# Token records with the head innermost, 576 bytes stored and gathered instead of 784

## The chip, the core and the metric

One core of a Trainium2 chip runs the whole program. The metric is the device time of one execution in microseconds: 197.95 us is the median of three runs of the kernel before (197.73 to 199.84). TensorE (PE) multiplies matrices and transposes, VectorE (DVE) and ScalarE (ACT) work on elements, GpSimd (POOL) issues indirect transfers here, and SyncE (SP) issues plain ones. DMA queues move data between the memory of the chip (DRAM) and the core's own memory (SBUF); TensorE writes its results to PSUM, 128 partitions of eight banks.

## The reference

A linear attention over random sketches is followed by a mixture of experts with one expert per token. There are 4 batches of 1088 tokens, 4 heads of 32 numbers, 64 sketch features, so 4352 tokens of 128 numbers; 8 experts of hidden width 1024. All is float32.

```
def phi(x):                                   # 8 x 8 = 64 features per head
    a = einsum('rd,bhsd->bhsr', S1, x); b = einsum('rd,bhsd->bhsr', S2, x)
    return outer(a, b)
q_p, k_p = phi(q), phi(k)
kv = einsum('bhsf,bhsd->bhfd', k_p, v); z = sum(k_p, axis=2)
attn = einsum('bhsf,bhfd->bhsd', q_p, kv) / (einsum('bhsf,bhf->bhs', q_p, z) + 1e-06)
x = attn as [4352, 128]
logits = x @ w_gate; e = argmax(logits); gate = softmax(logits)[e]
eom = sigmoid(x @ w_output_gate)
out = gate * eom[e] * (relu(x @ w1[e]) @ w2[e])
```

## The kernel before, in words

Tokens go in 34 chunks of 128, in nine groups (eight of four chunks, the last of two), and the groups in three routes of 12, 12 and 10 chunks. For each group TensorE makes the sketches, VectorE the products, and TensorE either adds the keys' part up per batch (`sums`) or turns the queries' part (`turned`) and multiplies it with the batch's sums (`attend`). Next to the 32 sums of a head stand the denominator and 16 gate logits, so that a head has VG = 49 numbers and a token W = 4 x 49 = 196. ScalarE copies these from PSUM into `xall` (`below`: one copy per pair of heads at L595, the denominator with its epsilon at L596). VectorE then takes the reciprocal of the denominators in place (L608), scales the logits (L610) and adds the four heads up (L612, L613): `shared`. When a route is whole, VectorE chooses experts and slots (`choose_first`, `choose_second`, `slot`), ScalarE makes the exponentials, VectorE the weight of the token (`weigh`), and `label` (L739) writes that weight into the record over its first logit, at column VZ = 33. `store` (L743) sends the route's records, all 196 columns of each token, to a DRAM table `xt` of 784 bytes per token.

The expert part works in tiles of 128 rows of one expert. GpSimd gathers a tile's records from `xt` by a list of row numbers into a buffer of `xin` (`fetch`, L858); a gather needs the stores of the routes that it may read and the list (`index_fixed`, which ends at L717). VectorE multiplies the sums by the reciprocal (`divide`, L868, into `xdiv`), TensorE turns the tile (`turn`, L872), VectorE copies it (`turn_copy`), TensorE multiplies up (`up`, L885), ScalarE or VectorE takes the positive part (`relu`), TensorE multiplies down (`down`, L899), ScalarE scales by the record's weight (`scale`, L902), and GpSimd scatters the rows to the output (`give`, L998). Sixteen tiles are done alone, after the first and second route. Then three tiles per expert are done as one group of up to 384 columns (`group_divide` L929 and L931, `group_up` L951, `group_down` L968 and so on), and a few last tiles follow, as many as there are rows left over, with weights fetched into buffers that are free by then.

The order of all this is written out by hand: the list `ORDER` names every step, and each engine runs its own steps in that order, each waiting by semaphores for what it needs. Names that matter below: `Rg` is `below` of group g (ScalarE), `Xg` is `shared`, `CAi`, `CBi`, `WEi`, `LAi`, `STi` lead from a route's logits to its store, `IXm` ends a list of rows, `Ft` is a gather, `XDt` a division, `TNt` a turn, `UPt` a multiplication up. Around the first route ScalarE has `R1`, `R2` one behind the other, and VectorE has `X1 X2 CA0 Mq.5 CB0 Mk.5 Pk.5 Mq.6 WE0 LA0` (the `M` and `P` steps belong to later groups' sketches). TensorE has `TN0`, the first turn, right behind the sums of group 5. PSUM buffers go round: two pairs of banks (`ps_w`) serve sketches, turned queries, the sums for `below`, and the multiplications up, so `UP2` takes the buffer that `R8` gives back.

Of the kernel before, what the change touches and what calls it, by code (L numbers as in the profile page):

```python
# [12 lines left out]
F32 = mybir.dt.float32  # L13
# [4 lines left out]
ACTF = mybir.ActivationFunctionType  # L18
# [6 lines left out]
TS = 128  # L25
# [33 lines left out]
JOINED = ()  # L59
# [28 lines left out]
def kernel(  # L88
# [27 lines left out]
    W = H * VG  # L116
    JT = (N + (len(MARKS) + 1) * TS) // TS
# [8 lines left out]

    xt = dram.tile([N, W], F32, tag="xt", name="xt")

# [173 lines left out]
    xins = const("xin", [TS, NX + 3, W])  # L302
# [72 lines left out]
    for t in xin:  # L375
        blank(t, 2, W // 2)
# [7 lines left out]
    lgs = Ring("lg", 1, [128, 16 * max([1] + [len(x) for x in JOINED]), 2 * E])  # L384
# [199 lines left out]
    def sums_of(g):  # L584
        cs = groups[g]
        return xall[:, cs[0]:cs[-1] + 1].rearrange("p c (k x) -> p (c k) x", x=VG)
# [4 lines left out]
    def below(g):  # L591
        n = 2 * len(groups[g])
        out = sums_of(g).rearrange("p (k h) x -> p h k x", h=2)
        for b in range(2):
            nc.scalar.copy(out[:, b], now["nd", g][:, b, :n])  # L595
        nc.scalar.activation(out[:, :, :, D], now["nd", g][:, :, :n, D], ACTF.Identity, bias=eps)  # L596
        ps_w.back(("nd", g))

    def shared(g):
        i = route_of[g]  # L600
        cs = range(groups[joined(g)[0]][0], groups[g][-1] + 1)
        n = len(cs)
        at = cs[0] - routes[i][0]
        if at == 0:
            now["x", i], now["L", i] = xall[:, routes[i][0]:routes[i][-1] + 1], Ls()
        raw = xall[:, cs[0]:cs[-1] + 1].rearrange("p c (k x) -> p (c k) x", x=VG)
        rc = raw[:, :, D]
        nc.vector.reciprocal(rc, rc)  # L608
        lg = lgs()[:, :4 * n]
        nc.vector.tensor_mul(lg, raw[:, :, VZ:], rc.unsqueeze(2).to_broadcast((128, 4 * n, 2 * E)))  # L610
        pairs = lg.rearrange("p (c a k) e -> p c a k e", a=2, k=2)
        nc.vector.tensor_add(pairs[:, :, 0], pairs[:, :, 0], pairs[:, :, 1])  # L612
        nc.vector.tensor_add(now["L", i][:, at:at + n], pairs[:, :, 0, 0], pairs[:, :, 0, 1])  # L613
# [123 lines left out]
    def label(i):  # L737
        n, x = len(routes[i]), now["x", i]
        nc.vector.tensor_mul(x[:, :n, VZ], now["co", i][:, :n], now["ey", i][:, :n, E + 1])  # L739

    def store(i):
        a, n = routes[i][0], len(routes[i])
        nc.sync.dma_start(xt[a * 128:(a + n) * 128].rearrange("(c p) w -> p c w", p=128), now["x", i])  # L743
# [122 lines left out]
    def divide(t):  # L866
        x = xin[room(t)].rearrange("p (k x) -> p k x", x=VG)
        nc.vector.tensor_mul(xdiv[t % 2].rearrange("p (k d) -> p k d", d=D), x[:, :, :D], x[:, :, D].unsqueeze(2).to_broadcast((TS, H, D)))  # L868
# [32 lines left out]
    def scale(t):  # L901
        nc.scalar.activation(at_ys(t), now["y", t], ACTF.Copy, scale=xin[room(t)][:, VZ:VZ + 1])  # L902
        ps_y.back(t)
# [22 lines left out]
    def group_divide(e):  # L926
        x = xins[:, room(first_of(e)):room(first_of(e)) + TG]
        heads = x.rearrange("p t (k x) -> p t k x", x=VG)
        nc.vector.tensor_mul(wide_div.rearrange("p (t k d) -> p t k d", t=TG, d=D), heads[:, :, :, :D],  # L929
                             heads[:, :, :, D].unsqueeze(3).to_broadcast((TS, TG, H, D)))  # L930
        nc.vector.tensor_copy(scales[e % 3], x[:, :, VZ])  # L931
# [235 lines left out]
    def scale_last(t):  # L1167
        nc.vector.tensor_scalar_mul(at_ys(t), now["y", t], xin[room(t)][:, VZ:VZ + 1])
        ps_y.back(t)
# [95 lines left out]
```

## Time and profile before

| | |
|---|---|
| runs | 197.95 us median (197.73 to 199.84) |
| profiled execution | 200.12 us, of which the span of the trace is 198.4 |
| mean granted TensorE clock | 0.983 |
| busy: PE, PEld | 187.1, 169.6 us (94%, 85%) |
| busy: DVE, ACT, POOL | 110.1, 72.8, 89.4 us (56%, 37%, 45%) |
| DMA | 31.11 MB, mean 157 GB/s |
| indirect queue (gathers and scatters) | 5.65 MB, 9.8% of 16 engines |
| SP's queue (q1, with the stores) | 16.44 MB, 24.1% |

PE is the time of matrix instructions, PEld that of loading their stationary operand. Times in the trace count from the start of the span. A group of instructions is named by its line, its engine and the tiles that it writes and reads. The chain of waits is followed back from the last instruction of the run, at each step to what released it; where an engine was simply busy, the step is the instruction before it on the same engine.

### The profile page before, as it was taken

What the parts mean: (1) busy time and instruction counts of PE and PEld (TensorE: products, weight loads), DVE (VectorE), ACT (ScalarE), POOL (GpSimd) and SP (SyncE); (2) the same over time, 40 slices, a digit from 0 to 9 for tenths busy, and PEclk for the clock granted to TensorE, in tenths of its full rate; (3) what the DMA queues carried; (4) which work ended last, traced back from release to release, by engine and by line L of the source; (5) the groups of instructions that cost most, each with busy time, mean ns of one, the idle gap of its engine ahead of it and who ended that gap; (6) DMA issues with size and microseconds to landing.
All of it is one profiled execution on the core that took longest, in us unless ns stands there. A gap on an engine that the chain in (4) does not pass through costs nothing.

```text
span 198.4 us, 5595 instructions
## 1 busy us (share of the span) xinstructions
PE 187.1 (94%) x2207; PEld 169.6 (85%) x2207; DVE 110.1 (56%) x299; ACT 72.8 (37%) x173; POOL 89.4 (45%) x117
## 2 busy tenths in 40 slices
PE   7999999795899999999999999999999999999980
PEld 6999998695899999999999996777988876788980
DVE  5579889984856848548453842342642806155230
ACT  7526685635257634333022304031242121223300
POOL 1830000007806105776057877758677375145071
PEclk9999999999799999999999999999999999999996
DMA  5969875354588699556999422122111110001010
GB/s 153 335 190 326 282 241 167 99 151 149 143 304 324 188 342 274 188 180 159 405 423 420 160 59 63 49 57 72 41 45 47 24 44 13 18 17 43 14 33 28
DMA packets 14878, 31.11 MB, mean 157 GB/s; under 512 B 2553, under 2 KB 7815, under 8 KB 14064
## 3 DMA queue, kind: packets, MB, share of 16 engines
q1 hardware_dynamic: 9328, 16.44, 24.1%
q10 hardware_dynamic: 2320, 8.39, 13.1%
q0 software_dynamic: 3184, 5.65, 9.8%
q8 instruction: 31, 0.51, 1.1%
q14 instruction: 15, 0.12, 0.2%
HBM read 25.53 MB, written 5.90 MB: 158 GB/s over the span
## 4 chain that ended last, share of the span: by engine, by line
DMA 44%; PE 40%; issue 7%; POOL 4%; DVE 2%; ACT 1%; POOLq 1%; DVEq 0%
DMA xin<-xt,putf 18%; DMA out_dram<-ys,putf 14%; PE w L885 11%; DMA xin<-xt,putfar 8%; PE t L431 6%; PE y L899 6%; PE acc L899 4%; DMA xt<-xall 4%; PE w L556 4%; PE w L579 3%; PE acc L497 3%; POOL xin L858 3%; PE w L417 2%; POOL out_dram L998 1%; PE t L872 1%
## 5 line engine op out<-in xcount | busy, mean ns | idle before, releaser
L858 POOL DMA_INDIRECT xin<-xt,putf x36 | 39.2, 1089 | 52.3 <-ACT ab L452 33.5
L998 POOL DMA_INDIRECT out_dram<-ys,putf x36 | 36.6, 1017 | 42.7 <-ACT ys L902 12.2
L885 PE MATMUL w<-xsT,wt 128*128 128x128 f32 x256 | 32.4, 284 | 0.0
L951 PE MATMUL w<-vt,wt 128*128 128x256 f32 (+5 forms) x128 | 32.3, 396 | 0.0
L885 PEld LDWEIGHTS w<-xsT,wt 128*128 128x128 f32 x256 | 31.2, 201 | 0.0
L951 PEld LDWEIGHTS w<-vt,wt 128*128 128x128 f32 x128 | 22.7, 190 | 6.0 <-DVE kT L957 0.4
L957 DVE TENSOR_SCALAR kT<-w 128x768 f32<-128x768 f32 x8 | 7.7, 958 | 32.9 <-PE w L951 32.9
L890 ACT ACTIVATE hT<-w 128x1024 f32<-128x1024 f32 x13 | 13.3, 1022 | 20.9 <-PE w L885 20.9
L899 PE MATMUL y<-wt,hT 128*128 128x128 f32 x144 | 17.7, 276 | 0.0
L899 PEld LDWEIGHTS y<-wt,hT 128*128 128x128 f32 x144 | 16.8, 192 | 0.1
L968 PE MATMUL acc<-kT,wt 128*128 128x256 f32 (+5 forms) x64 | 16.2, 396 | 0.1
L968 PE MATMUL acc<-qT,wt 128*128 128x256 f32 (+5 forms) x64 | 16.0, 392 | 0.0
L972 ACT COPY kT<-acc 128x384 f32<-128x384 f32 x8 | 3.8, 478 | 31.0 <-PE acc L968 31.0
L968 PEld LDWEIGHTS acc<-kT,wt 128*128 128x128 f32 x64 | 11.6, 190 | 3.6 <-issue 0.7
L968 PEld LDWEIGHTS acc<-qT,wt 128*128 128x128 f32 x64 | 11.8, 190 | 2.9
L899 PE MATMUL acc<-wt,hT 128*128 128x128 f32 x112 | 13.7, 275 | 0.0
L899 PEld LDWEIGHTS acc<-wt,hT 128*128 128x128 f32 x112 | 13.1, 192 | 0.0
L959 ACT ACTIVATE qT<-w 128x768 f32<-128x768 f32 x8 | 6.5, 810 | 14.0 <-PE w L951 14.0
L878 DVE COPY xsT<-t 128x128 f32<-128x128 f32 x19 | 5.4, 286 | 10.8 <-PE t L872 10.8
L465 DVE TENSOR_TENSOR kp<-ab 128x1024 f32<-128x1024 f32 (+1 forms) x9 | 10.5, 1166 | 0.7 <-PE acc L497 0.3
L497 PE MATMUL acc<-vt,kp 128*64 128x33 f32 (+1 forms) x288 | 10.6, 224 | 0.0
L465 DVE TENSOR_TENSOR qp<-ab 128x1024 f32<-128x1024 f32 (+1 forms) x9 | 10.4, 1161 | 0.2
(182 smaller groups left out, 292.6 us busy)
## 6 DMA issues: line engine op xcount, KB each, us to landing
wt<-in_w_dram ACTq DMA_DIRECT2D x16, 512.0 KB, 5.6
xall<-in_w_dram SPq DMA_DIRECT2D x3, 1024.0 KB, 9.8
xt<-xall SPq DMA_DIRECT2D x2, 1176.0 KB, 9.7
vt<-in_v_dram SPq DMA_DIRECT2D x8, 260.0 KB, 4.5
kT<-in_k_dram SPq DMA_DIRECT2D x8, 256.0 KB, 4.3
qT<-in_q_dram SPq DMA_DIRECT2D x8, 256.0 KB, 4.4
qp<-in_w_dram SPq DMA_DIRECT2D x1, 1024.0 KB, 6.7
qpT<-in_w_dram SPq DMA_DIRECT2D x1, 1024.0 KB, 13.9
```

Source lines behind the costliest of these rows:

```text
L431: nc.tensor.matmul(ps[:, j].rearrange("p i x -> p (i x)"), src[:, j * 128:(j + 1) * 128], Sb.rearrange("p i h x -> p (i h x)"), start=True ...
L465: nc.vector.tensor_mul(res[:, :n], bview(av, [list(av.ap[1]), list(av.ap[2]), [0, r]]), bview(bv, [list(bv.ap[1]), [0, r], list(bv.ap[2])]))
L497: nc.tensor.matmul(now["acc", b][64 * h:64 * (h + 1), s], kp[p0:p0 + n, heads_at("k", g, j, s) + h].rearrange("s i j -> s (i j)"), now["v" ...
L556: nc.tensor.transpose(ps[:, :, x], block(x), ident)
L858: nc.gpsimd.indirect_dma_start(out=xin[room(t)], out_offset=None, in_=xt[:n, :], in_offset=bass.IndirectOffsetOnAxis(ap=index(t), axis=0), ...
L885: nc.tensor.matmul(ps[:, c], w[:, c], x[:, own(t)], start=True, stop=True)
L890: nc.scalar.activation(out, now["h", t], ACTF.Relu)
L899: nc.tensor.matmul(ps, h[:, c], w[:, c], start=(c == 0), stop=(c == FC - 1))
L951: nc.tensor.matmul(now["h", "g", e, s][:, c, :n], w[:, s * (FC // 4) + c], x[:, :n], start=True, stop=True)
L957: nc.vector.tensor_scalar_max(wide_h[s], src, 0.0)
L968: nc.tensor.matmul(ps[:, :n], w[:, c], wide_h[c // (FC // 4)][:, c % (FC // 4), :n], start=(c == 0), stop=(c == FC - 1))
L998: apart("out", nc.gpsimd.indirect_dma_start(out=out, out_offset=bass.IndirectOffsetOnAxis(ap=index(t), axis=0), in_=at_ys(t), in_offset=No ...
```

## The change

The record's 4 x 49 numbers are laid with the head innermost: column 4 x + k holds number x of head k. So the 128 sums come first, then the four denominators (RC, columns 128 to 131), then the 64 logits, and the weight of the token is written at column WZ = 132. A row of `xt` is cut at WR = 144 columns, 576 bytes, which holds the sums, the denominators and the weight, and eleven logits that nobody reads. `xall` keeps 196 columns per token, as the logits are needed there. The gather's buffers `xin` have 144 columns.

What follows from that: `below` writes each pair of heads to columns that lie four apart; the reciprocals of a chunk are four neighbours; `shared` multiplies blocks of 16 x 4 and adds over the innermost index; `divide` and `group_divide` read the sums of one head four columns apart; `store` takes 144 of the 196 columns. `turn`, `up` and everything behind them have the layout that they had. `ORDER` is not touched.

```diff
+    WR = 144
+    RC, WZ = slice(H * D, H * VZ), H * VZ
...
-    xt = dram.tile([N, W], F32, tag="xt", name="xt")
+    xt = dram.tile([N, WR], F32, tag="xt", name="xt")
...
-    xins = const("xin", [TS, NX + 3, W])
+    xins = const("xin", [TS, NX + 3, WR])
...
-        blank(t, 2, W // 2)
+        blank(t, 2, WR // 2)
...
 def sums_of(g):
-        return xall[:, cs[0]:cs[-1] + 1].rearrange("p c (k x) -> p (c k) x", x=VG)
+        return xall[:, cs[0]:cs[-1] + 1].rearrange("p c (x k) -> p c k x", k=H)
...
 def below(g):
-        out = sums_of(g).rearrange("p (k h) x -> p h k x", h=2)
+        out = sums_of(g).rearrange("p c (s h) x -> p h c s x", h=2)
+        src = now["nd", g][:, :, :n].rearrange("p h (c s) x -> p h c s x", s=2)
         for b in range(2):
-            nc.scalar.copy(out[:, b], now["nd", g][:, b, :n])
-        nc.scalar.activation(out[:, :, :, D], now["nd", g][:, :, :n, D], ACTF.Identity, bias=eps)
+            nc.scalar.copy(out[:, b], src[:, b])
+        nc.scalar.activation(out[:, :, :, :, D].rearrange("p h c s -> p c s h"), src[:, :, :, :, D].rearrange("p h c s -> p c s h"),
+                             ACTF.Identity, bias=eps)
...
 def shared(g):
-        raw = xall[:, cs[0]:cs[-1] + 1].rearrange("p c (k x) -> p (c k) x", x=VG)
+        raw = xall[:, cs[0]:cs[-1] + 1].rearrange("p c (x k) -> p c x k", k=H)
         rc = raw[:, :, D]
         nc.vector.reciprocal(rc, rc)
-        lg = lgs()[:, :4 * n]
-        nc.vector.tensor_mul(lg, raw[:, :, VZ:], rc.unsqueeze(2).to_broadcast((128, 4 * n, 2 * E)))
-        pairs = lg.rearrange("p (c a k) e -> p c a k e", a=2, k=2)
-        nc.vector.tensor_add(pairs[:, :, 0], pairs[:, :, 0], pairs[:, :, 1])
-        nc.vector.tensor_add(now["L", i][:, at:at + n], pairs[:, :, 0, 0], pairs[:, :, 0, 1])
+        lg = lgs()[:, :n]
+        nc.vector.tensor_mul(lg, raw[:, :, VZ:], rc.unsqueeze(2).to_broadcast((128, n, 2 * E, H)))
+        nc.vector.tensor_add(lg[:, :, :, :2], lg[:, :, :, :2], lg[:, :, :, 2:])
+        nc.vector.tensor_add(now["L", i][:, at:at + n], lg[:, :, :, 0], lg[:, :, :, 1])
...
 def label(i):
-        nc.vector.tensor_mul(x[:, :n, VZ], now["co", i][:, :n], now["ey", i][:, :n, E + 1])
+        nc.vector.tensor_mul(x[:, :n, WZ], now["co", i][:, :n], now["ey", i][:, :n, E + 1])
...
 def store(i):
-        nc.sync.dma_start(xt[a * 128:(a + n) * 128].rearrange("(c p) w -> p c w", p=128), now["x", i])
+        nc.sync.dma_start(xt[a * 128:(a + n) * 128].rearrange("(c p) w -> p c w", p=128), now["x", i][:, :, :WR])
...
 def divide(t):
-        x = xin[room(t)].rearrange("p (k x) -> p k x", x=VG)
-        nc.vector.tensor_mul(xdiv[t % 2].rearrange("p (k d) -> p k d", d=D), x[:, :, :D], x[:, :, D].unsqueeze(2).to_broadcast((TS, H, D)))
+        x = xin[room(t)]
+        nc.vector.tensor_mul(xdiv[t % 2].rearrange("p (k d) -> p k d", d=D), x[:, :H * D].rearrange("p (d k) -> p k d", k=H),
+                             x[:, RC].unsqueeze(2).to_broadcast((TS, H, D)))
...
 def group_divide(e):
-        heads = x.rearrange("p t (k x) -> p t k x", x=VG)
-        nc.vector.tensor_mul(wide_div.rearrange("p (t k d) -> p t k d", t=TG, d=D), heads[:, :, :, :D],
-                             heads[:, :, :, D].unsqueeze(3).to_broadcast((TS, TG, H, D)))
-        nc.vector.tensor_copy(scales[e % 3], x[:, :, VZ])
+        nc.vector.tensor_mul(wide_div.rearrange("p (t k d) -> p t k d", t=TG, d=D), x[:, :, :H * D].rearrange("p t (d k) -> p t k d", k=H),
+                             x[:, :, RC].unsqueeze(3).to_broadcast((TS, TG, H, D)))
+        nc.vector.tensor_copy(scales[e % 3], x[:, :, WZ])
```

The two scalings, `scale` and `scale_last`, take the weight from column WZ instead of VZ.

## Rows read from the trace of the kernel before

**Rows 1.** The page: busy tenths of TensorE in 40 slices.

```profile
PE   7999999795899999999999999999999999999980
```

**Rows 2.** The waits of PE: line, waited for: us in total, times, longest.

```profile
PE t L872 <- DVE xdiv L868: 2.8, 1, 2.8
```

**Rows 3.** The chain that ended last, at five places: start, us, what.

```profile
37.24 6.97 DMA xt<-xall
...
45.14 4.79 DMA xin<-xt,putf
...
50.30 0.33 PE t L872
...
51.85 5.17 PE w L885 x32
...
93.13 3.57 PE w L885 x32
```

**Rows 4.** The timeline, 27.8 to 43 us: start, us, engine, line, operation.

```profile
27.81 0.88 ACT L595 COPY xall<-w 128x392 f32<-128x392 f32 x2 [0.46 <-PE w L579]
...
28.89 0.87 ACT L595 COPY xall<-w 128x392 f32<-128x392 f32 x2
...
29.79 0.29 ACT L596 ACTIVATE xall<-w,eps 128x16 f32<-128x16 f32 x1
...
30.26 0.25 DVE L608 RECIPROCAL xall<-xall 128x16 f32<-128x16 f32 x1
...
34.63 1.23 DVE L465 TENSOR_TENSOR kp<-ab 128x1024 f32<-128x1024 f32 x1
...
36.22 0.27 DVE L732 TENSOR_REDUCE ss<-ey 128x12 f32<-128x108 f32 x1
...
42.73 0.17 DVE L717 SCALAR_TENSOR_TENSOR putf<-valf,nonef 128x8 int32<-128x8 f32 x1
```

**Rows 5.** Stretches: length, busy PE PEld DVE ACT POOL, granted clock, DMA share, GB/s.

```profile
38.40:39.60 1.20, 0.30 (x1) 0.11 (x1) 1.10 (x3) 1.13 (x7) 0.00 (x0) 1.00 0.98 319
...
30.00:40.00 10.00, 8.65 (x211) 7.93 (x211) 9.21 (x30) 6.19 (x20) 0.00 (x0) 1.00 0.43 133
...
100.00:105.00 5.00, 5.00 (x47) 5.00 (x46) 2.48 (x10) 0.98 (x3) 3.07 (x3) 1.00 1.01 419
...
51.80:52.00 0.20, 0.20 (x3) 0.20 (x2) 0.20 (x1) 0.20 (x1) 0.01 (x1) 0.50 0.00 0
```

**Rows 6.** Groups of instructions by line and form: count, busy us, mean ns.

```profile
L595 ACT COPY xall<-w 128x392 f32<-128x392 f32 x16 | 7.0, 493 | 4.7 <-PE w L579 4.7
...
L595 ACT COPY xall<-w 128x196 f32<-128x196 f32 x2 | 0.6, 328 | 1.2 <-PE w L579 1.2
...
L641 DVE TENSOR_TENSOR oh<-t,first 128x96 f32<-128x96 f32 x2 | 0.6, 317 | 0.0
...
L627 DVE TENSOR_TENSOR ex<-mx,L 128x96 f32<-128x96 f32 x2 | 0.5, 260 | 0.1
```

**Rows 7.** Instructions of single lines: ns shortest, median, longest, starts, forms.

```profile
L372 ACT COPY xin<-ys x12: 348/349/350, 3.8 to 6.6; 128x196 f32<-128x196 f32 x12
...
L636 ACT COPY oh<-bumped x2: 198/201/204, 59.3 to 74.9; 128x8 f32<-128x8 f32 x2
...
L596 ACT ACTIVATE xall<-w,eps x9: 273/289/291, 23.2 to 72.5; 128x16 f32<-128x16 f32 x8, 128x8 f32<-128x8 f32 x1
...
L715 DVE TENSOR_TENSOR valf<-rows_of x3: 173/174/200, 42.3 to 100.2; 128x8 f32<-128x8 f32 x2, 128x24 f32<-128x24 f32 x1
L715 DVE TENSOR_TENSOR valfar<-farboth x1: 192/192/192, 155.6 to 155.6; 128x32 f32<-128x32 f32 x1
...
L610 DVE TENSOR_TENSOR lg<-xall x9: 291/425/427, 23.8 to 75.8; 128x256 f32<-128x256 f32 x8, 128x128 f32<-128x128 f32 x1
```

**Rows 8.** The timeline at 63 us: a last copy and the weights after it.

```profile
63.34 0.27 ACT L596 ACTIVATE xall<-w,eps 128x8 f32<-128x8 f32 x1
...
63.66 1.86 PEld L885 LDWEIGHTS w<-xsT,wt 128*128 128x128 f32 x16
```

More of the change, by code (lines that the diff above doesn't have):

```diff
@@ L116 @@
     W = H * VG
+    WR = 144
+    RC, WZ = slice(H * D, H * VZ), H * VZ
+    assert WZ < WR <= W
     JT = (N + (len(MARKS) + 1) * TS) // TS
@@ L383 @@
     kvs = Ring("kv", 2, [128, 2, D])
-    lgs = Ring("lg", 1, [128, 16 * max([1] + [len(x) for x in JOINED]), 2 * E])
+    lgs = Ring("lg", 1, [128, 4 * max([1] + [len(x) for x in JOINED]), 2 * E, H])
     Ls = Ring("L", 2, [128, RG, 2 * E])
@@ L901, in scale @@
     def scale(t):
-        nc.scalar.activation(at_ys(t), now["y", t], ACTF.Copy, scale=xin[room(t)][:, VZ:VZ + 1])
+        nc.scalar.activation(at_ys(t), now["y", t], ACTF.Copy, scale=xin[room(t)][:, WZ:WZ + 1])
         ps_y.back(t)
@@ L1167, in scale_last @@
     def scale_last(t):
-        nc.vector.tensor_scalar_mul(at_ys(t), now["y", t], xin[room(t)][:, VZ:VZ + 1])
+        nc.vector.tensor_scalar_mul(at_ys(t), now["y", t], xin[room(t)][:, WZ:WZ + 1])
         ps_y.back(t)
```

## The prediction, made before the changed kernel was run

> **What bounds the kernel now.** I read the page first. TensorE's busy tenths stand at 9 in almost every slice; the one deep dip, a 5, is the slice from 44.6 to 49.6 us, with a 7 two slices before it [rows 1]. From 50 us on the tenths say that TensorE runs without a hole until the end, so work saved on another engine, a queue or a transfer after that point buys nothing unless TensorE waits for it. The waits of PE name the dip: 2.8 us, once, for the first division at L868 [rows 2]. The chain of waits says what was late: the first store of records is issued at 37.24 and lands 6.97 us later, the first gather is issued at 45.14 and takes 4.79 us, then come the division and, at 50.30, its transpose on TensorE [rows 3]. So a change to the records counts there, and there alone: where does the first transpose come, and does anything later make TensorE wait that did not wait before?
>
> The timeline shows what sets the issue of that store. It is not ScalarE's copies of group 3, which the chain names; that store holds groups 0 to 2. ScalarE copies group 1 from 27.81 and group 2 from 28.89, ending with L596 at 29.79 + 0.29 = 30.08; VectorE takes group 2 at 30.26 (L608), then goes on through the choice, a product (34.63) and the weights (36.22) to the label before the store [rows 4]. VectorE is busy 9.21 of these 10 us (the stretch 30 to 40) [rows 5], and its operations stand in one fixed order, so I count whatever delays L608 of group 2 as delaying the store by the same amount.
>
> **The change, part by part.**
>
> *The store, shorter.* Twelve chunks of 128 tokens are 1536 rows, 96 on each of 16 engines, 784 bytes before and 576 after. In the bulk of it the engines move 319 GB/s, all busy (share 0.98), where long weight rows move 419 [rows 5]. So one row takes 784 x 16 / 319 = 39.3 ns, of which 29.9 are bytes at the faster rate and 9.4 belong to the row. A row of 576 bytes then takes 22.0 + 9.4 = 31.4: 7.9 ns saved x 96 = 0.76 us; in proportion to bytes alone it is 1.0. I take 0.9. Ends: nothing, if the row is the price and not its bytes; and 0.265 x 6.97 = 1.8 if the whole time to landing shrinks, of which only 1.33 can be used, since the indices of the first gather are ready at 42.73 + 0.17 = 42.90 [rows 4] against the landing at 44.21.
>
> *The first gather, shorter.* 128 rows, 27 KB less, at 319 GB/s: 0.08, so -0.1 us; ends 0 and 0.3 (a share of the time in which it competes with a weight load). Gathers and stores after it are waited for by no TensorE instruction: nothing, covered by TensorE's own queue of work after 50 us [rows 1]; if that cover went, each would give another gain, not a loss.
>
> *ScalarE's copies out of the sums (L595).* The same 392 numbers per copy, but written 16 bytes apart, where before 49 lay side by side. No row shows a step of 16 bytes, so I bound it. ScalarE's ordinary price per number is (493 - 328) / 196 = 0.84 ns [rows 6]. Its writes in long steps: L636 writes 8 numbers 52 bytes apart in 201 ns, where the fixed part is 349 - 196 x 0.84 = 184, so 2.1 ns each; L596 goes from 273 to 289 ns for 8 more numbers in steps of 196 bytes, 2.0 each [rows 7]. That is 1.25 ns a number on top, from very small instructions. VectorE, per number: (425 - 291) / 128 = 1.05 ns [rows 7]; L715 over 24 numbers 20 bytes apart takes 200 ns, over 32 side by side 192 [rows 7], so 24 side by side would take 184, and the step costs 16 / 24 = 0.7 ns a number. L641, which writes 52 bytes apart, takes 317 where L627 takes 260, 0.6 a number over 96 [rows 6]. Ends: 0 and 1.25 (ScalarE's own rows); nothing below zero, since no number is left out. I take 0.7, because 20 bytes is the nearest step to 16. So a copy takes 0.27 us longer, a group's pair 0.55.
>
> [...] The rows at 20, 52 and 196 bytes agree that long steps cost; no row before the change shows 16.
>
> *What waits behind these copies.* Group 1's end moves by 0.55, group 2's by 1.10, to 31.18. VectorE's group 1 starts 0.55 later, so its group 2 could start at 30.81; ScalarE is later, at 31.18, which is +0.92. The last addition (L613) reads 64 numbers in steps of 16 bytes, +0.05. The store's issue: **+1.0** (ends 0 and, with 1.25 ns, copies of +0.49, group 2 done at 32.04, +1.8). TensorE waits somewhat too for the product at 34.63, later by the same 1.0; that moves its work toward the dip at 47.5, which has 2.8 us to give.
>
> *Divisions.* L868 reads its 128 numbers 16 bytes apart: +0.09 each. The first is on the path, and so is the second, whose transpose comes with no room; the other 17 and the eight wide ones (+0.27 each) run a tile ahead of TensorE, so nothing.
>
> *The last, short group.* At 63.34 + 0.27 = 63.61 ScalarE ends a short group, whose buffer TensorE fills from 63.66 [rows 8]: no more than 0.05 to spare. Two copies of 196 numbers, +0.14 each, make TensorE wait **+0.2** (at 1.25 ns, with the group behind it, up to 0.9).
>
> *Costed at nothing.* Blanking 144 columns instead of 196 (L372, ScalarE ahead of its first copies), the reciprocal and the product at L610 (runs of 64 and of 4 side by side), the label, the scales: same counts, off the path. No DMA is added or moved and no queue is reordered; SP and POOL issue what they did.
>
> Sum: +1.0 (issue) - 0.9 (store) - 0.1 (gather) + 0.1 + 0.1 (two divisions) + 0.2 (short group) = **+0.4 us**. It is made on the profiled execution, 200.12 us around a span of 198.4, so 200.5 there; that execution stands 2.2 above the median, 197.95, on which I put the same difference: **198.3 us**.
>
> **The rivals.**
>
> *The step is nearly free, a small gain.* The copies keep their 493 ns, so the issue stays at 37.24. For it: 16 bytes is shorter than any step in the rows. Against: 20 bytes costs 0.7. Then -0.9 - 0.1 = -1.0: 196.9.
>
> [...]
>
> *Slower: ScalarE becomes the bound ahead of the first store.* Its place is the copies of groups 1 and 2; its price 1.25 ns a number, +1.8 at the issue; and the store is bound by its rows, so it gives nothing back. With +0.2 for divisions and 0.5 for the short group: +2.5, 200.4. At that price it passes 1% when the store saves less than 0.5. For it: ScalarE's only rows with long steps, both at 2 ns. Against: they are instructions of 8 and 16 numbers, and 319 against 419 GB/s says that bytes weigh more than rows.
>
> *It does not do what it says*, the transfer being cut into the same packets by another rule: counted in the last case.
>
> **How the numbers follow.** Forecast 0.50, its own range 197.5 to 199.6 (price 0.4 to 1.25); small gain 0.17; clock holds 0.20; slower 0.13. Over or under 1%, 1.98 us, is about what a measurement tells from no change. So faster 0.20, same 0.67, slower 0.13. The range takes in the forecast, the small gain and the clock's case, and cuts off most of the slower case: 195.2 to 200.1.
>
> **What would show it.** L595 at about 760 ns (free: 493; dear: 980). The first store issued near 38.2 and landing in about 6.1 us. L868 near 370 ns. The PE wait for L868 near 2 us, and the clock after it at 0.50 or at 1.00. A TensorE wait of 0.2 before L885 at 63 us. I am wrong if L595 does not move, if the store's time does not, if the clock stays up, or if TensorE finds a new wait after 64 us.

## The result, and the profile after

The changed kernel takes 200.66 us (median of 19 runs, 198.43 to 204.0), the kernel before, measured beside it, 198.23 (19 runs, 196.62 to 200.01). The ratio is 1.011, with a 95% interval of 1.0077 to 1.0142: about 2.2 us lost. A ratio here compares only those executions of either kernel that lie within 1.5% of its fastest, so it isn't quite the ratio of the medians. The forecast was 198.3, and its range ended at 200.1.

The profile is of the slowest of these executions, 204.0 us around a span of 202.3. First its page, TensorE's busy tenths and its granted clock in 40 slices of 5.06 us each.

```profile
PE   7999997899999999999999999999999999999990
...
PEclk9999999955579999999999999999999999999998
```

The dip of [rows 1] is gone: there is no slice with a 5, but the ninth to twelfth slices hold a clock of 5 to 7, where TensorE is busy nine tenths of the time and more. Stretches of the same execution show where that begins (columns as in [rows 5]).

```profile
40.00:42.00 2.00, 1.36 (x39) 1.17 (x43) 1.90 (x5) 1.19 (x8) 0.00 (x0) 0.67 0.98 298
42.00:50.00 8.00, 8.00 (x138) 7.33 (x130) 4.69 (x11) 3.04 (x6) 2.80 (x2) 0.50 0.08 22
50.00:57.00 7.00, 7.00 (x134) 6.80 (x133) 3.45 (x12) 3.10 (x8) 5.24 (x5) 0.50 0.46 130
```

The clock is at 0.50 from about 41 to 57 us; before, it was at 1.00 over 40 to 50 us, until the wait was over, 0.91 over 50 to 52, and at 0.50 only behind it [rows 5]. So this execution is late early: the products for the third expert, whose weights TensorE loads at 63.66 before [rows 8], start 4.3 us later here. The first line is of before, the second of after.

```profile
63.71 2.00 PE L885 MATMUL w<-xsT,wt 128*128 128x128 f32 x16
...
68.03 2.01 PE L890 MATMUL w<-xsT,wt 128*128 128x128 f32 x16
```

The groups by line and form (the columns of [rows 6]) give the prices of the new layout.

```profile
L599 ACT COPY xall<-w 128x392 f32<-128x392 f32 x16 | 12.7, 907 | 6.6 <-PE w L582 6.6
L872 DVE TENSOR_TENSOR xdiv<-xin 128x128 f32<-128x128 f32 x19 | 7.0, 378 | 3.6 <-PE t L877 3.6
L933 DVE TENSOR_TENSOR vt<-xin 128x384 f32<-128x384 f32 x8 | 6.7, 838 | 0.5 <-DMA xin<-xt,putf 0.4 <-PE t L941 0.2
...
L617 DVE TENSOR_TENSOR L<-lg 128x64 f32<-128x64 f32 x8 | 2.2, 275 | 0.3
...
L599 ACT COPY xall<-w 128x196 f32<-128x196 f32 x2 | 0.9, 556 | 1.2 <-PE w L582 1.2
```

L599 is L595 of before: 907 ns where [rows 6] has 493, and 556 where it has 328. That is 414 / 392 = 1.06 ns a number on top, and 228 / 196 = 1.16 in the small form. L872 (before: L868, 283 ns) is 95 ns longer over 128 numbers, 0.74 each.

The timeline from 27 to 47 us answers to [rows 4].

```profile
27.70 1.61 ACT L599 COPY xall<-w 128x392 f32<-128x392 f32 x2 [0.40 <-PE w L582]
...
29.52 1.60 ACT L599 COPY xall<-w 128x392 f32<-128x392 f32 x2
...
31.45 0.25 DVE L613 RECIPROCAL xall<-xall 128x16 f32<-128x16 f32 x1 [0.46 <-ACT xall L600]
...
38.35 0.38 SPq L747 DMA_DIRECT2D xt<-xall  x1
...
45.66 0.17 DVE L721 SCALAR_TENSOR_TENSOR putf<-valf,nonef 128x8 int32<-128x8 f32 x1
46.73 1.79 POOL L862 DMA_INDIRECT xin<-xt,putf  x1 [35.46 <-DVE ab L460]
```

A pair of copies takes 1.6 us where it took 0.88; group 2's reciprocal starts 1.19 later (30.26 before), the store is issued 1.11 later (37.24 before). The index list stands at 45.83, 2.93 later than before, and the gather follows it by 0.90: in this execution the list, not the store, is what comes last. The waits of PE name a wait that was not there before, and no longer the one of [rows 2].

```profile
PE t L434 <- DVE ab L460: 1.3, 1, 1.3
```

It ends at 34.42: the product Sk.7 needs a buffer that VectorE's addition L460 gives back, and that addition stands behind the reciprocal and the choice for group 2.

### The profile page after: what moved, and what is told of

Read it like the earlier page. It is cut to its first block, busy times and chain, and to the rows that moved or that the text cites. A ratio compares the mean times of both kernels' runs of the same rounds, so it can differ in the third digit from the quotient of the medians.

```text
span 202.3 us, 5595 instructions
## 1 busy us (share of the span) xinstructions
PE 192.8 (95%) x2207; PEld 174.7 (86%) x2207; DVE 115.0 (57%) x299; ACT 78.2 (39%) x173; POOL 90.5 (45%) x117
## 4 chain that ended last, share of the span: by engine, by line
PE 45%; DMA 36%; issue 6%; POOL 5%; DVE 3%; ACT 3%; POOLq 1%; DVEq 0%
DMA xin<-xt,putf 14%; DMA out_dram<-ys,putf 14%; PE w L890 10%; DMA xin<-xt,putfar 8%; PE t L434 6%; PE y L904 5%; PE acc L500 5%; PE w L582 5%; PE w L559 4%; PE acc L904 4%; POOL xin L862 3%; PE w L420 2%; POOL out_dram L1002 2%; ACT xall L599 2%; PE t L877 1%
## 5 line engine op out<-in xcount | busy, mean ns | idle before, releaser
L862 POOL DMA_INDIRECT xin<-xt,putf x36 | 40.6, 1128 | 53.6 <-DVE ab L460 35.5
L890 PE MATMUL w<-xsT,wt 128*128 128x128 f32 x256 | 31.4, 278 | 0.0
L890 PEld LDWEIGHTS w<-xsT,wt 128*128 128x128 f32 x256 | 30.1, 195 | 0.1
L599 ACT COPY xall<-w 128x392 f32<-128x392 f32 (+1 forms) x18 | 13.6, 868 | 7.8 <-PE w L582 7.8
L500 PE MATMUL acc<-vt,kp 128*64 128x33 f32 (+1 forms) x288 | 12.3, 242 | 0.3 <-issue 0.3
L500 PEld LDWEIGHTS acc<-vt,kp 128*64 128x64 f32 (+1 forms) x288 | 11.3, 159 | 0.9 <-issue 0.3
L582 PE MATMUL w<-kz,qpT 64*64 64x49 f32 x544 | 11.7, 239 | 0.3 <-issue 0.2
```

The lines of the kernel that those rows point to most:

```text
L500: nc.tensor.matmul(now["acc", b][64 * h:64 * (h + 1), s], kp[p0:p0 + n, heads_at("k", g, j, s) + h].rearrange("s i j -> s (i j)"), now["v" ...
L582: nc.tensor.matmul(ps[64 * t:64 * (t + 1), h, 2 * j + s], now["qT", g][64 * h:64 * (h + 1), 2 * j + s, 64 * t:64 * (t + 1)], kz[(c * 128 + ...
L599: nc.scalar.copy(out[:, b], src[:, b])
L862: nc.gpsimd.indirect_dma_start(out=xin[room(t)], out_offset=None, in_=xt[:n, :], in_offset=bass.IndirectOffsetOnAxis(ap=index(t), axis=0), ...
L890: nc.tensor.matmul(ps[:, c], w[:, c], x[:, own(t)], start=True, stop=True)
```

## The theories

**Theory 1, the path.** The longer copies hold VectorE, VectorE holds the store and TensorE, and by either the first gather comes later; the shorter store can't make up for it. **Theory 2, the clock.** The path comes out even, as predicted, and the loss is TensorE's clock falling near 41 us, some 10 us earlier than before. **Rival 3.** The strided divisions are what costs.

There were five series of runs. In the first four the executions of every kernel, the one before included, took 211 to 231 us, with holes on TensorE behind 60 us (single ones up to 7.1 us) that neither the trace of the kernel before nor those of series 5 have. So their whole times are read only roughly, and their traces only up to the first experts. In series 5 the kernel before took 198.28. "Line" below means one least-squares fit of all executions of a set of series: a constant for each series and kernel, and one slope for the mean granted clock that each execution lists; the ± is 1.96 standard errors.

| series | kernel | median us (runs) | before us (runs) | ratio, 95% |
|---|---|---|---|---|
| 1 | after2 | 225.0 (8) | 224.62 (11) | |
| 1 | layout_only | 225.82 (6) | | |
| 1 | short_only | 225.09 (6) | | |
| 1 | order_m5 | 225.94 (6) | | |
| 2 | packed | 217.44 (12) | 221.75 (30) | 0.992, 0.987 to 0.997 |
| 2 | short_slow | 217.35 (6) | | 0.989, 0.979 to 0.999 |
| 2 | after3 | 219.14 (12) | | 0.990, 0.979 to 1.000 |
| 2 | short_only2 | 217.64 (12) | | |
| 3 | after4 | 221.83 (6) | 225.05 (10) | |
| 3 | packed2 | 221.15 (6) | | |
| 3 | layout_only2 | 226.56 (6) | | |
| 3 | short_only3 | 221.02 (8) | | |
| 4 | after5 | 219.85 (12) | 222.06 (24) | 1.018, 1.008 to 1.028 |
| 4 | after_filled | 221.7 (6) | | 1.012, 0.999 to 1.025 |
| 4 | before_filled | 220.87 (12) | | 1.012, 0.991 to 1.034 |
| 4 | packed_filled | 215.61 (6) | | 0.982, 0.968 to 0.996 |
| 5 | after6 | 199.77 (12) | 198.28 (23) | 1.006, 0.999 to 1.013 |
| 5 | packed_filled2 | 197.79 (12) | | 0.996, 0.990 to 1.001 |

## The halves of the change

**The layout alone**: the changed kernel with all 784 bytes stored and gathered.

```
-    WR = 144
+    WR = W
```

> The changed kernel with rows of 784 bytes stored and gathered as before (WR = W): the layout without the shorter transfer. Theory 1: the same wait of 1.3 us at 33 us, the store issued at the same 38.4 but about 1 us longer, so that the first division is waited for again by 1 to 3 us; ratio to before 1.010 to 1.020, above that of the change. Theory 2: clock as in the changed kernel and the ratio as there, 1.007 to 1.014.

> The head-innermost layout with all 784 bytes stored and gathered. Theory 1: as slow as the changed kernel within 0.3% (ratio 1.004 to 1.015), since the bytes saved are behind the list of rows anyway. The prediction's theory (store last for the first gather) would put it 0.9 us or more above the changed kernel, a ratio near 1.01 where the changed kernel's is 1.005. Wait of 1.3 us ahead of Sk.7 in either.

The timeline of layout_only, the list and the first gather:

```profile
44.88 0.17 DVE L721 SCALAR_TENSOR_TENSOR putf<-valf,nonef 128x8 int32<-128x8 f32 x1
45.95 1.80 POOL L862 DMA_INDIRECT xin<-xt,putf  x1 [34.68 <-DVE ab L460]
```

The gather is again 0.90 behind the list, though the store carries as many bytes as before; the wait of 1.3 us ahead of Sk.7 is there in both traces. So the wait comes with the layout, and where the list is last, the bytes of the store don't matter. How late the list is, is not the layout's alone here: TensorE, which makes part of the list, was slow ahead of it in this execution: 62 products of L582 took 1.68 us from 41.61, where 63 of short_only's L579 took 1.14 from 40.01, at a clock of 1.00.

**The short record alone**: the kernel before, its store and gathers cut to the first 144 numbers (the fourth head's numbers then reach no expert; the amount of work is unchanged).

```
-    xt = dram.tile([N, W], F32, tag="xt", name="xt")
+    xt = dram.tile([N, 144], F32, tag="xt", name="xt")
```

> The kernel before with rows cut to 144 columns and the old layout, so that the transfer is short and the copies are not touched; it leaves out the records' last columns, so the fourth head's numbers reach no expert. Theory 1: copies 493 ns, the store lands 0.7 to 1.0 us earlier, the wait for the first division is 1.8 to 2.1 us instead of 2.8; ratio 0.993 to 0.997. Theory 2: the same on the path; if the clock holds, 0.985 to 0.99.

> The kernel before with rows cut to 144 columns once more. Theory 1: first gather issued near 44.1, first turn near 48.5 with a wait of 1 us instead of 2.8; ratio 0.985 to 0.995. Theory 2: the same, and at the lower end where the clock holds.

> The kernel before with records cut to their first 576 bytes in the store and the gathers (the fourth head's numbers reach no expert; work and layout are as before). Theory 1: no wait ahead of Sk.7, the first gather ahead of the kernel before's by about 1 us, a ratio of 0.990 to 0.998. Theory 2: the same ratio as the changed kernel where the clocks are alike.

Its chain, as in [rows 3]:

```profile
37.12 6.00 DMA xt<-xall
...
44.05 3.74 DMA xin<-xt,putf
...
48.54 0.33 PE t L872
...
50.03 0.88 ACT xall L595 x2
...
51.27 3.84 PE w L885 x32
```

The store takes 6.00 instead of 6.97, the gather 3.74 instead of 4.79, and the first transpose comes 1.76 us earlier than in [rows 3]; no wait at 33 us. The prediction's store term (-0.9) is borne out here, its gather term (-0.1) was too small. What is late next shows too: the chain then passes through ScalarE's copies for a later group, and the first expert starts only 0.58 us earlier (51.27 against 51.85). The whole times don't show the gain by themselves: 225.09 against 224.62 in series 1, but 217.64 against 221.75 and 221.02 against 225.05 in series 2 and 3.

Over series 1 to 4 (205 executions) the line puts the short record alone at 1.1 ± 0.9 us faster than the kernel before at equal clock, the layout alone at 1.5 ± 1.3 slower, and the whole change, between them, at 0.5 ± 0.8 slower. By these, the change is a gain and a loss of about the same size.

## Which part of the layout costs

**Longer copies without the layout**: the short record above, with a dummy copy of 343 (or 98) numbers by ScalarE ahead of each copy; VectorE reads runs, as before.

```
+            m = 7 if n == 8 else 2
+            nc.scalar.copy(slack[:, :m], now["nd", g][:, b, :m])
```

> The kernel before with rows cut to 144 columns (the fourth head's numbers reach no expert), and one more ScalarE copy of 343 numbers (98 in the last group) ahead of each copy out of the sums, into a tile that nobody reads: the price of the copies with neither the layout nor its divisions. Theory 1: as the changed kernel: a wait of about 1.3 us at 33 us, the list of rows ready at 45 or later, the first gather 0.9 behind the list and not behind the store; ratio 1.005 to 1.014. A rival 3 (the strided divisions cost it): as with the rows cut alone, 0.985 to 0.995.

Its waits of PE:

```profile
PE t L431 <- DVE ab L457: 1.2, 1, 1.2
```

The wait ahead of Sk.7 is back at 1.2 us, with no strided write and no strided read in the kernel: ScalarE's time alone makes it. The copies begin at 27.90, as in short_only (27.82), and the store's issue comes at 38.44, 1.32 later, the gather at 45.34, 1.29 later. Rival 3 isn't needed for either. The whole time doesn't follow, though: Theory 1 asked for a ratio of 1.005 to 1.014 and for a gather behind the list; the ratio is 0.989, inside the range given for Rival 3, and the gather comes 1.08 behind the list (which stands at 44.26), more than the 0.90 seen where the list is last. In the same series the changed kernel itself stands at 0.990, so this series doesn't tell the kernels apart by their copies, and what the strided divisions cost in the whole time isn't shown by it.

**The wait taken away**: in the changed kernel, the addition that gives the buffer back is put ahead of group 2's count.

```
-... X1 X2 CA0 Bk.5 Bq.5 Mq.5 TC4 ...
+... X1 X2 Bk.5 Bq.5 Mq.5 CA0 TC4 ...
```

> The changed kernel with one step of VectorE's order moved: the addition of group 5's queries (Mq.5), for whose buffer TensorE waits at 33 us, is put ahead of the choice of the first route (CA0). Theory 1: the wait falls from 1.3 to 0.2 to 0.4 us, the store is issued 0.3 later; TensorE comes about 1 us earlier to the first turn and the ratio to before is 1.002 to 1.008. Theory 2: no change of the ratio where the clock falls at 40 us as before; 0.995 to 1.0 where it holds.

The timeline of order_m5:

```profile
32.09 0.25 DVE L613 RECIPROCAL xall<-xall 128x16 f32<-128x16 f32 x1 [0.45 <-ACT xall L600]
...
39.01 0.39 SPq L747 DMA_DIRECT2D xt<-xall  x1
...
45.73 0.17 DVE L721 SCALAR_TENSOR_TENSOR putf<-valf,nonef 128x8 int32<-128x8 f32 x1
...
46.80 1.80 POOL L862 DMA_INDIRECT xin<-xt,putf  x1 [35.50 <-DVE ab L460]
```

The wait of 1.3 us is gone, and nothing comes earlier: from the reciprocal to the gather it is 14.71 us, against 15.28 in the profile after, with its clock at 0.50 from about 41 us, and 14.15 in after6 below, at 1.00 (order_m5's clock was 0.66 from 40 to 45 us). The time, 225.94, is not better than after2's 225.0, though with 6 and 8 runs so far apart that says little. So nothing shows that wait by itself to be the loss; as the trace reads, VectorE's order only gives the delay to somebody else.

**The same bytes, laid in runs**: 576 bytes, but each head's 33 sums side by side and the 16 logits of each head behind them, so that ScalarE writes and VectorE reads runs.

```
+            nc.scalar.copy(out[:, b], src[:, b, :, :, :VZ])
+            nc.scalar.copy(lout[:, b], src[:, b, :, :, VZ:])
```

> The short record with the heads outermost: 4 x 33 sums and denominators in front, then 4 x 16 logits, so that 576 bytes are stored and gathered, and nothing is written or read 16 bytes apart; ScalarE has two copies per pair of heads, 33 and 16 numbers wide, instead of one. Theory 1, as the trace of the layout alone has sharpened it (the copies hold VectorE, VectorE holds TensorE at 33 us, and TensorE's order holds the list of rows, which is then later than the store): the four copies of a group together about 1.1 us, the wait at 33 us at most 0.5, the list ready near 43.3, the first gather issued at 44.1 to 44.5, the first turn at 48.5 to 49.3; ratio 0.988 to 0.997. Theory 2 (clock alone): no better than the changed kernel unless the clock holds.

> The 576-byte record with each head's 33 numbers side by side and the logits behind them (ScalarE writes runs, VectorE reads runs). Copies of some 0.5 us plus a short one for the logits, no wait ahead of Sk.7, list of rows within 0.3 us of the kernel before's, first gather ahead of it by 1 to 1.7 us, the clock's first fall not before 50 us. Theory 1: a ratio of 0.990 to 0.997 against the kernel before, since the first gather is earlier by 1 to 1.7 us and half of that comes through. Theory 2: the same as the short record with the layout as it was, wherever the clock falls at the same place.

Packed has no wait at 33 us, issues its first gather at 43.47 and starts the first transpose at 48.28, 2.0 earlier than [rows 3]; the time is 0.8% under the kernel before (series 2, where after3, with the strided copies, is at 0.990 too). In packed2 the clock fell in that execution:

```profile
41.00:47.00 6.00, 6.00 (x72) 5.33 (x67) 3.79 (x10) 1.86 (x8) 2.42 (x2) 0.50 0.07 19
```

So the early fall needs neither the strided copies nor the wait at 33 us: it came in packed2, in short_only3 (0.50 over 41 to 47 us) and partly in short_only2 (0.74 over 40 to 45), which have neither, and it stayed away in after3, after4, after5 and after6 (1.00 over 40 to 50), which have both.

## Is it the clock?

The remaining changed kernels of series 1 to 4 are repeats of the change beside the others.

> The changed kernel once more, for a trace beside the others. Theory 1 (ScalarE's longer copies hold VectorE, and VectorE holds TensorE at 33 us): the first copies out of the sums near 907 ns, the wait of TensorE for VectorE's addition (L460) again about 1.3 us, the store issued near 38.4, and the first division no longer waited for, or by less than 1 us; ratio to before 1.007 to 1.014. Theory 2 (the path is even, and the difference is TensorE's clock alone): the clock at its lower level for clearly more than the 3.5 us of before, from some point before 50 us; where it isn't, the time is that of before.

> The changed kernel beside the others on the same chip. Theory 1: ratio 1.007 to 1.014, the wait at 33 us 1.3, first gather issued 0.9 behind the list of rows, 45.9 to 46.8. Theory 2: the same time as the kernel before in executions whose granted clock is alike.

> The changed kernel once more, beside the three kernels below. Where the granted clock stays at 1.00 from 30 to 50 us, the trace should show a wait of 1.2 to 1.3 us ahead of the products for Sk.7, the list of rows about 1 us later than in the kernel before, the first gather issued 0.9 us behind the list (not behind the store's landing), and the chain's first transpose within 1 us of the kernel before's. Theory 1 (the slower copies hold VectorE, VectorE holds TensorE, the list is then the last thing the gather needs) puts the whole time at a ratio of 1.004 to 1.012; Theory 2 (the path is even and only an earlier fall of the clock costs) puts it at 1.00 in executions whose clock holds and at 1.01 or more in those whose clock falls before 50 us.

After2's clock fell at 40 us (0.59 over 40 to 42, 0.50 over 42 to 50) and its first transpose came at 58.96; in after3 and after4 the clock held at 1.00 over 40 to 50 us and it came at 49.41 and 49.99, no later than the 50.30 of [rows 3]. That was the best evidence for Theory 2. It shows as well that the list of rows can be last without any fall of the clock. The lines are of after3:

```profile
43.01 0.17 DVE L721 SCALAR_TENSOR_TENSOR putf<-valf,nonef 128x8 int32<-128x8 f32 x1
...
44.09 1.80 POOL L862 DMA_INDIRECT xin<-xt,putf  x1 [33.00 <-ACT xall L600]
```

The gather is 0.91 behind the list, and 0.90 and 0.91 in after4 and after5. The ratios expected for after3 and after4 did not come: 0.990 in series 2, and a median under the one of before in series 3.

The next kernels fill TensorE's idle time with products that nobody reads.

```
+    def busy(n):
+        for i in range(n):
+            nc.tensor.matmul(ps_y.tiles[0][:, :128], ident, ident, start=True, stop=True)
```

> The changed kernel beside its filled form. Path theory: ratio 1.004 to 1.012 against the kernel before, the same as the filled form within 0.3%. Clock theory: slower than its filled form by 0.5 to 1.5%, with a mean granted clock lower by 0.01 or more.

> The changed kernel with products of the identity by itself, into a bank of PSUM that is free until the first expert's second product: 8 ahead of Sk.7 (in its new wait of 1.3 us) and 3 ahead of each of the two products of the third batch's gates (in its waits of 0.5 us at 40 us). Nothing that is used is computed by them. Clock theory: the clock stays at 1.00 to 50 us in the trace, the mean granted clock of the runs is higher by 0.01 to 0.02 than the changed kernel's, the time lower by 0.5 to 1.5%, and the ratio to the kernel before about 1.00. Path theory: no difference beyond 0.3%.

> The kernel before with 3 such products ahead of each of the two products of the third batch's gates (it has no wait at 33 us). Clock theory: it gains as well, 0.3 to 1%, since its own clock falls near 41 us in some executions. Path theory: no change beyond 0.3%.

> The 576-byte record with the heads outermost, with the same 6 products. Either theory puts it ahead of the kernel before, by 0.5 to 1.5%; the clock theory puts it ahead of the plain packed record too.

In after_filled TensorE has no idle time at all from 30 to 45 us, and the clock holds:

```profile
30.00:45.00 15.00, 15.00 (x361) 14.42 (x361) 12.62 (x38) 10.58 (x28) 0.00 (x0) 1.00 0.35 104
```

It is not clearly faster for it: the medians are 221.7 us against 219.85 for the plain changed kernel beside it, the ratios 1.012 against 1.018 with intervals that overlap, and Theory 2 asked for 0.5 to 1.5% less. So this pair doesn't decide. Before_filled changed nothing that can be told; its expectation that the kernel before falls to the lower clock near 41 us has no trace behind it, as the one trace of that kernel holds 1.00 until 51 us. Packed_filled was the fastest of its series.

Series 5 is the one with times near those of the result.

> The changed kernel. Clock theory: over executions with a mean granted clock within 0.01 of each other the two kernels differ by less than 1 us, and the trace reaches the third expert's first product at 63 to 64 us where the clock holds to 50 us, at 67 us or later where it falls near 41 us. Path theory: the changed kernel is 1.5 to 2.5 us slower at the same clock.

> The 576-byte record with the heads outermost and the six products in TensorE's gaps. Third expert's first product at 61 to 62 us with the clock held to 50 us, a ratio of 0.975 to 0.995 against the kernel before.

After6's 12 executions had a mean granted clock of 0.990, the 23 of the kernel before 0.984: the changed kernel had the better clock and was slower, 199.77 against 198.28. The line through series 5 puts it at 1.9 ± 0.9 us slower at equal clock. Theory 2 said less than 1 us, Theory 1 said 1.5 to 2.5. So in series 5 Theory 2 falls as the only cause, by a narrow margin, and the 0.5 ± 0.8 of series 1 to 4 would have allowed it. The clock explains how far the single executions lie apart (one hundredth of clock goes with 1.2 ± 0.4 us), and what happened in the profile after. It also has a share in the first measurement: there the 19 executions of the changed kernel had a mean clock of 0.978, against 0.990 in series 5, which at that slope is 1.5 us; their mean times differ by 1.3. The clocks of the kernel before are not on record there; if it had its 0.984 of series 5, about 0.8 of the 2.2 us is clock, by this estimate.

After6's profile is of an execution whose clock was 0.999, so its chain of waits is the path itself. It can be laid beside [rows 3].

```profile
26.72 1.07 issue
...
28.20 1.61 ACT xall L599 x2
...
30.11 1.49 ACT xall L599 x2
...
31.93 0.26 DVE xall L613
...
38.83 6.32 DMA xt<-xall
...
46.08 4.50 DMA xin<-xt,putf
...
51.05 0.33 PE t L877
...
52.64 3.57 PE w L890 x32
```

The chain runs through the two pairs of copies, then VectorE piece by piece without a hole to the store, then the gather: the very path that the prediction named. Measured from the start of group 1's copies, 28.20 (27.81 before; ahead of it stands a hole of 1.07 us to which the profile gives no cause), the store's issue is at +10.63, before +9.43: 1.20 longer. The store is 0.65 shorter, gather and first division together 0.19. The sum to the first transpose is +0.36. The two waits of PE that matter:

```profile
PE t L877 <- DVE xdiv L872: 1.7, 1, 1.7
...
PE t L434 <- DVE ab L460: 1.3, 1, 1.3
```

TensorE's new wait of 1.3 us is paid out of the old one, which goes from 2.8 [rows 2] to 1.7: in this execution it costs nothing, since the list, at 44.76, is ready before the store lands at 45.15.

```profile
44.59 0.17 DVE L721 SCALAR_TENSOR_TENSOR putf<-valf,nonef 128x8 int32<-128x8 f32 x1
```

The margin is 0.4 us, and in after3 to after5 the list was last. There the first transpose came 22.38 to 23.10 us behind the start of group 1's copies, against 22.49 before and 22.85 in after6: the path is longer by 0.3 us in the mean of the four, where the prediction's terms up to there make 0.1. Behind the first experts stands the short group. The first line is of before, the others are of after6:

```profile
62.75 0.55 ACT L595 COPY xall<-w 128x196 f32<-128x196 f32 x2 [1.20 <-PE w L579]
```

```profile
61.94 0.88 ACT L599 COPY xall<-w 128x196 f32<-128x196 f32 x2 [1.20 <-PE w L582]
62.86 0.27 ACT L600 ACTIVATE xall<-w,eps 128x8 f32<-128x8 f32 x1
...
63.21 0.31 PE L582 MATMUL w<-kz,qpT 64*64 64x49 f32 x2 [0.41 <-issue]
```

From the first copy to the end of L600 it takes 1.19 us; before, the copies began at 62.75 and L596 ended at 63.61, 0.86. But in after6 TensorE doesn't wait for L600, which ends at 63.13: it has a hole of 0.41 ahead of the last two products of L582, these two take 0.31 us where the 94 ahead of them took 1.61, and it reaches the third expert 2.42 us after the first of these products (61.19 to 63.61), against 1.71 before (62.00 to 63.71). The price of the short group is seen where that hole is absent, in after2, layout_only, layout_only2 and after_filled; the line is of layout_only2:

```profile
72.99 0.19 PEld L890 LDWEIGHTS w<-xsT,wt 128*128 128x128 f32 x1 [0.33 <-ACT xall L600]
```

From 63.6 on the traces run side by side: what starts at 93.13 in [rows 3] starts at 93.08. But the trace of before had lost 1.6 us to the clock behind its wait (5.17 us for 32 products [rows 3]), and after6 nothing (3.57). At equal clock after6 is 1.5 us behind: 0.39 at the start, 0.36 to the first transpose, 0.08 to the first expert (51.05 to 52.48, against 50.30 to 51.65), 0.71 around the hole of 0.41.

Neither hole is made by the strided layout. A hole stands ahead of the same last 73 products of L582 in before_filled, short_only, short_slow, packed2 and packed_filled2 (0.19 to 0.67 us), and ahead of the same last two in short_only, its two repeats, short_slow and packed (0.44 to 0.56). The second was in none of the four traces with rows of 784 bytes and in 11 of 16 with 576, counting packed_filled2, where it stands twelve products earlier; whether it belongs to the short record isn't shown.

**The best version.** Packed_filled2 takes the store off the chain altogether. Its chain, and its copies by form:

```profile
42.14 0.56 PE t L715 x12
...
43.49 0.18 DVE putf L731
...
44.56 4.73 DMA xin<-xt,putf
...
49.66 0.33 PE t L887
```

```profile
L606 ACT COPY xall<-w 128x264 f32<-128x264 f32 x16 | 6.4, 398 | 5.2 <-PE w L588 5.2
...
L607 ACT COPY xall<-w 128x128 f32<-128x128 f32 x16 | 4.6, 288 | 0.0
```

Two copies, 686 ns together, write what L599 writes in 907, in runs. The gather now waits for the list of rows that TensorE made, and the store, shorter and issued in time, lands before. It takes 197.79 us: 2.0 under the changed kernel with the same bytes. Against the kernel before it is 0.996 (0.990 to 1.001), and by the line, at equal clock, 0.3 ± 0.9 us slower: no gain over the kernel before is shown here. Its expectation, 0.975 to 0.995 with the third expert at 61 to 62 us, was missed (that came at 62.37). A gain stands in series 4 (0.982 for packed_filled, where after5 is at 1.018) and in series 2, where the changed kernel gained as much.

## Why the prediction was wrong

*The path.* Right: the copies, VectorE without a hole, the store, the gather and the first transpose are the chain of after6; in after3 to after5 the list of rows, which the prediction had ready in time, came last instead. The wait for the first division was put near 2 us and is 1.7.

*The price of a step of 16 bytes.* This is the term that was mis-sized. "I take 0.7, because 20 bytes is the nearest step to 16": that row was of VectorE, and the instruction is ScalarE's. ScalarE's own rows, at 2 ns a number, were set aside as very small instructions. Measured: 1.06 ns on ScalarE, near the end that I called dear (1.25), and 0.74 on VectorE, where 0.7 was taken for the divisions. So the store's issue moved by 1.20 instead of 1.0, the short group by 0.33 instead of 0.2. That is 0.3 us; the forecast was off by about 1.8, so this step alone doesn't carry the miss.

*The store.* -0.9 forecast, -0.65 in after6, -0.97 in short_only. In after6 the bulk of it moves 284 GB/s:

```profile
40.00:41.20 1.20, 0.34 (x3) 0.11 (x1) 1.10 (x3) 1.04 (x7) 0.00 (x0) 1.00 0.91 284
```

A row of 576 bytes then takes 576 x 16 / 284 = 32.5 ns against the 39.3 of 784 bytes: 6.8 x 96 = 0.65 us. But the engines' share is 0.91 here and was 0.98 before [rows 5], so this isn't the price of a row alone, and the 0.9, taken without a row, lies between the two measurements. (The 1.33 that the prediction gives for the usable part is 44.21 - 42.90 = 1.31.)

*The sum.* With the sizes of after6 the prediction's own addition gives 1.20 - 0.65 - 0.19 + 0.08 (from the first transpose to the first expert, 1.43 against 1.35) + 0.33 = +0.8 us instead of +0.4. The measured loss is 2.4 between the medians of the first measurement, 1.5 in series 5, 1.9 ± 0.9 at equal clock. So some 0.7 to 1.6 us are not in the sum. About 0.8 of the first measurement is clock, by the estimate above, and is in no term of the sum. After6's 1.5 at equal clock hold 0.4 on the path; the rest is the later start and the hole at 62.80, which hides the short group's 0.33. Both holes come in kernels without the strided layout too, so the cause of what the change loses at equal clock beyond 0.8 stays open.

*The step costed at nothing.* TensorE's late product "moves its work toward the dip at 47.5, which has 2.8 us to give". This step failed too. It held in after6, by 0.4 us. In after3 to after5, at a clock of 1.00, the list that TensorE makes was last. In the profile after, at a clock of 0.50 from about 41 us, the dip has nothing left, the list is last, and the third expert is 4.3 us late. I had a rival in which the clock holds, and none in which it falls sooner: the sum put the lower clock of some executions at nothing. What sets off that fall is open: it came with and without the change.

*The slower rival* named the copies as the place and nearly their price (1.25 against 1.06) and gave 200.4; its condition, a store that saves less than 0.5, was not far off at 0.65. It had a chance of 0.13, and the range cut most of it off. *The clock holds* had a chance of 0.20, and the low end of the range, 195.2, leaves room for it: behind the wait the clock stays at 1.00, and the 1.6 us of [rows 3], where 32 products take 5.17 us and 3.57 later, are not lost. So it was in after6, where a wait of 1.7 us left the clock at 1.00 (50 to 60 us) and the 32 products took 3.57; yet the time was not lower, since the longer path and the two holes took as much. That a shorter or a split wait is what keeps the clock up isn't shown. *The free step* is refuted for this layout. Packed_filled2, which doesn't take the step at all, got -0.5 between medians and -0.9 by the ratio, but nothing at equal clock, so the -1.0 of this rival isn't shown there either. *That the change doesn't do what it says* is refuted: 864 KB are stored where 1176 were, and the store is shorter.

*The rest.* Divisions L872 at 378 ns (370 forecast), the wide ones at 838 against 551 ns, off the path as said. No new wait of TensorE behind 64 us in the profile after and in after6.

## What to carry to other kernels

Price a new access pattern by rows of the engine that will run it, even where they are small, and take a row of another engine as a bound at most: here a step of 16 bytes cost ScalarE 1.06 ns a number and VectorE 0.74. A record can be made shorter for the DMA without scattering the writes that fill it: lay runs, and give what was left over a second, short copy. Before a shorter transfer is counted, look for what comes last once it is short: here it was 0.4 us away in one execution, in the list of rows, and already last in others.

## What the runs showed of the hardware

ScalarE, copying float32 from PSUM to steps of 16 bytes in SBUF, took 1.06 ns a number more than to runs of 49 (907 against 493 ns for 392), and 1.16 in the small form (556 against 328 for 196); VectorE, reading steps of 16 bytes, 0.74 to 0.80 more (378 against 283 ns for 128; L617's 275 against L613's 224 before for 64). So the step of 16 bytes cost on both engines; the runs give its size and not its cause.

TensorE's granted clock was 1.00 from 38 to 40 us in the profile after, in after2, layout_only2, packed2 and short_only3, and 0.50 to 0.54 from 42 to 44; in order_m5 and short_only2 it was 0.66 and 0.74 in the mean from 40 to 45 us, and 1.00 from 45 to 50. It was 1.00 from 40 to 50 us in the kernel before, short_only, packed, short_slow, after3 to after6, after_filled, packed_filled and packed_filled2. The same kernel is on both sides of that. How busy TensorE was doesn't tell them apart: 0.92 of the 2 us from 39 in the profile after, where the clock fell, and 0.92 of the 2 us from 38 in the kernel before, where it held. No view shown here tells what decides it.
